# A fused retention and feed-forward kernel: one more token block through a seven-product first matmul, another seven-product scheme for the second, and part of v scaled on GpSimd

## Chip, cores and metric

The kernel runs on one core of one Trainium2 chip. The metric is the device time of one execution in microseconds (us). Before the change it is the median of three runs.

## The reference

A retention layer (8 batches, 8 heads, 576 positions, head dimension 64) and behind it a feed-forward layer with an exact GELU:

```python
scores = scale * np.matmul(q, k.transpose(0, 1, 3, 2))
gamma = 1.0 - 2.0 ** (-5.0 - np.arange(H, dtype=np.float32))
rel = pos[:, None] - pos[None, :]
Dmat = np.where(rel >= 0, gamma[:, None, None] ** rel[None, :, :], 0.0)
attn_out = np.matmul(scores * Dmat[None, :, :, :], v)
x = attn_out.transpose(0, 2, 1, 3).reshape(B * S, H * D)        # 4608 x 512
h = x @ w_in                                                    # w_in 512 x 2048
g = 0.5 * h * (1.0 + erf(h / np.sqrt(2.0)))
out = g @ w_out                                                 # w_out 2048 x 512
```

All arrays come in float32; the kernel works in bfloat16 with float32 sums.

## The kernel before, in words

The 4608 tokens are nine blocks t = 0 to 8 of `TOK` = 512. The retention part is cut into 36 units of 128 tokens, four to a block. A unit goes through these steps: q, k and v are loaded by GpSimd's DMA queue (L318), q and k are transposed (`turn`, L482, on TensorE for the first seven groups, `turn_dma`, L492, by DMAs of SyncE's queue behind that), scores (`sc`, L516 to L535), decay mask on VectorE (`ret`, L554 and L558), the inner product (`o_ps`, L591 and L600), the product with the running state (L653), and the evacuation to `xT` (L672, or L456/L461 for first units). The state `u_ps` (L619) needs v scaled per head (`vh`): `scaled_v` does this on ScalarE for the 15 units listed in `BY_ACT` (eight instructions a unit, L572) and on VectorE for 21 units (one instruction, L575).

**First product** (x by w_in, then GELU). Blocks 0 to 5 use the plain form `mlp1` (L701, tile `hT`): 16 column groups of four matmuls, 64 matmuls of 512 columns a block. From block `FAST` = 6 on, `fast` (L966, tile `f`) does it by a Winograd form: of each pair of column groups four pieces j, of each piece seven products P1 to P7 with four matmuls of 256 columns, so 112 matmuls of 256 columns a block. Its operands are sums of x (`xs`, L939) and of w_in (`wi`, L924 to L926, and L931 in place); its results are joined by VectorE (L981, L985) and passed through GELU on ScalarE (L987, L991). P7 is kept in a float32 tile of its own, `p7`.

**Second product** (g by w_out). Block 0 is plain (`mlp2`, L746, tile `oT`). Blocks 1 to 8 use `part` (L885, tile `m`): seven products M1 to M7 in Strassen's form, each in four steps k of four matmuls of 256 columns. `sum_g` makes three sums of g for each of four pieces j (L782 and L786 with 1024 elements a partition, L784 with 512). `sum_w` makes five sums of w_out (L192 to L195). `after` copies and adds the finished products (L821, L826, L837, L846, L851, L456/L461/L463), and stores the block (`store`, L729).

**Order.** Everything is recorded into the engines' queues by one host loop (`fire` and the `while True` loop behind it). It keeps an estimate of each engine's time in `T`, asks which step is ready, and appends its instructions. So the order of each queue is fixed when the program is built, and on the chip an instruction waits only for its operands and for those ahead of it in its queue. The list `ORDER` gives the order of the loads on GpSimd's queue (`wi1 k1 wi0 io ...`), in which `dq2` to `dq4` (L299) are small GpSimd multiplications that make decay factors; the entries with a plus sign are delays that steer the host loop and issue nothing.

For the last block three products are cut into three pieces (`PIECES`) so that the last stores are small.

Of the kernel before, what the change touches and what calls it, by code (L numbers as in the profile page):

```python
# [9 lines left out]
FP32 = mybir.dt.float32  # L10
BF16 = mybir.dt.bfloat16
# [6 lines left out]
def kernel(  # L18
# [52 lines left out]
    FAST, ALL_FAST = 6, 6  # L71
    N_LD = 5
    N_QKT = 4
# [6 lines left out]
    HOLD = 9  # L80

# [6 lines left out]
    g_pool = ctx.enter_context(tc.tile_pool(name="g", bufs=1))  # L88
# [15 lines left out]
    def on(engine, dur, ready=0.0):  # L104
# [37 lines left out]
    def constants():  # L142
# [7 lines left out]
        far_at = on("dve", 0.55, at)  # L150
        nc.vector.tensor_scalar(ident, val, 0.0, None, op0=ALU.is_equal)
        on("dve", 0.35)
# [6 lines left out]

    N_NEAR, NEAR = 5, (0, 2, 4, 6, 1, 3, 5, 7)  # L160
# [27 lines left out]
    def sum_w(i):  # L188
        w = w_out_sb[i]
        s = w_sum[i] = const.tile([128, 5, 256], BF16, name=f"w_sum{i}")  # L190
        b11, b12, b21, b22 = w[:, 0, 0:256], w[:, 0, 256:512], w[:, 1, 0:256], w[:, 1, 256:512]
# [4 lines left out]
        ws_at[i] = on("dve", 1.05, land_out[i]) + SEM  # L196

# [87 lines left out]
    def load(what, i):  # L285
# [8 lines left out]
        if what == "dq":  # L294
# [6 lines left out]
            dq_at[i] = on("pool", 1.2, dq_at[i - 1])  # L301
# [23 lines left out]
    for x, keys in enumerate(zip(*HW_FIRST)):  # L325
        for n, (what, i) in enumerate(keys):
# [3 lines left out]
    ORDER = ("wi1 k1 wi0 io q1 v0 q2 k2 v1 wi2 v2 k3 wi3 q3 v3 wi4 wi5 wi6 k4 q5 k5 q4 v5 wi7 wo1 wo0 k6 v4 dq2 "  # L330
# [7 lines left out]
             "b21+6.0").split()  # L338

    BY_ACT = {int(x[1:]) for x in ORDER if x[0] == "a"}  # L340
    S_LATE = {int(x[1:].split("+")[0]): float(x.split("+")[1]) for x in ORDER if x[0] == "s"}
    B_LATE = {int(x[1:].split("+")[0]): float(x.split("+")[1]) for x in ORDER if x[0] == "b"}
    DVE_LAG, P_WAIT, HURRY = ({int(x[1:].split("+")[0]): float(x.split("+")[1]) for x in ORDER if x[0] == kind} for kind in "zpu")
    ORDER = [x for x in ORDER if x[0] not in "abszpu"]
# [76 lines left out]
    DRAIN = 0.25  # L421
    SEM = 0.12
# [140 lines left out]
    def scaled_v(i):  # L563
# [5 lines left out]
        by_act = i in BY_ACT  # L569
        if by_act:  # L570
            for h in range(H):
                nc.scalar.activation(vh[:, h, :], loaded[i][1][:, h, :], AF.Copy, scale=dv[:, h, ci:ci + 1])  # L572
            st[i]["V"] = on("act", 2.0, at) + SEM
        else:
            nc.vector.tensor_tensor(vh, loaded[i][1], dv[:, :, ci:ci + 1].to_broadcast([128, H, D]), op=ALU.mult)  # L575
            st[i]["V"] = on("dve", 0.685, at) + SEM
# [109 lines left out]
    def g_of(t, mm):  # L686
        return g_tiles[t, mm // 2][:, mm % 2] if t else g_tiles[t, mm // 2][mm % 2]

    def g_done(t, j):
        if t > 0 and all((t, 4 * j + x, ts) in g_at for x in range(4) for ts in range(4)):  # L690
            at = max(g_at[t, 4 * j + x, ts] for x in range(4) for ts in range(4)) - SEM
            for x in range(3):
                queued.append((at, x, sum_g, (t, j, x)))
# [654 lines left out]
```

## Time and profile before

| | before |
|---|---|
| median of 3 runs | 285.56 us (285.5 to 286.11) |
| span of the profiled execution | 283.7 us |
| median less that span | 1.9 us |
| TensorE matmuls busy | 278.0 us (98%) |
| VectorE busy | 199.7 us (70%) |
| ScalarE busy | 158.8 us (56%) |
| GpSimd busy | 114.0 us (40%) |
| matmuls | 3361 |

The profile gives no other time for the profiled execution than its span, from the first to the last instruction. What lies around it is taken as the 1.9 us between that span and the median. PE is TensorE's matmuls, PEld its weight loads, DVE VectorE, ACT ScalarE, POOL GpSimd, SP SyncE; a q behind the name means the engine's sequencer, which issues DMAs. In rows of the groups, "busy, mean ns of one | idle before" follow the count.

### The profile page before, as it was taken

How to read it: one execution, taken by the hardware profiler on the slowest of the kernel's cores; microseconds unless marked ns; L12 is line 12 of the kernel's file. 1: busy time of each engine (PE TensorE's matmuls, PEld its weight loads, DVE VectorE, ACT ScalarE, POOL GpSimd, SP SyncE). 2: the span in 40 equal slices, each digit the busy share in tenths (PEclk: the TensorE clock that was granted, in tenths of full speed). 3: DMA queues.
4: the chain of work that ended last, by engine and by line, in shares of the span. 5: the costliest groups of instructions: out<-in, count | busy, mean ns of one | idle time of the engine just before them, and what ended most of it. 6: DMA issues, size and time to landing. Idle time of an engine off the chain costs nothing.

```text
span 283.7 us, 8075 instructions
## 1 busy us (share of the span) xinstructions
PE 278.0 (98%) x3361; PEld 207.6 (73%) x3361; DVE 199.7 (70%) x412; ACT 158.8 (56%) x362; POOL 114.0 (40%) x143
## 2 busy tenths in 40 slices
PE   8989999999999999999999999999999999999994
PEld 3577666688874588548855778558888888888894
DVE  5753483979865595898178867889669968966822
ACT  5676724755456635693298874564565374665320
POOL 8979987993364465625468552000000000000000
PEclk9999999999999999999999999999999999999999
DMA  9999999999999999999999999910003000400133
GB/s 150 165 182 173 188 180 163 146 142 147 172 161 195 190 147 128 156 229 149 135 197 203 147 137 150 222 21 2 0 2 128 23 2 0 151 0 2 74 114 111
DMA packets 152804, 35.39 MB, mean 125 GB/s; under 512 B 141120, under 2 KB 148928, under 8 KB 152768
## 3 DMA queue, kind: packets, MB, share of 16 engines
q0 software_dynamic: 116832, 18.10, 95.3%
q1 hardware_dynamic: 34528, 16.26, 32.9%
q10 hardware_dynamic: 1408, 0.52, 0.7%
q8 instruction: 26, 0.43, 0.7%
q14 instruction: 10, 0.08, 0.1%
HBM read 36.70 MB, written 9.44 MB: 163 GB/s over the span
## 4 chain that ended last, share of the span: by engine, by line
PE 92%; POOL 3%; DMA 3%; issue 0%; DVE 0%; POOLq 0%
PE m L885 35%; PE hT L701 29%; PE f L966 13%; PE oT L746 5%; PE o_ps L600 3%; PE sc L535 3%; DMA w_in<-in_moe_w_in_dram 3%; POOL qk L318 2%; PE o_ps L653 1%; PE u_ps L619 1%; PE qk_ps L482 1%; POOL v_ld L318 1%; POOL w_in L291 1%; PE sc L525 0%; PE o_ps L591 0%
## 5 line engine op out<-in xcount | busy, mean ns | idle before, releaser
L701 PE MATMUL hT<-xT,w_in 128*128 128x512 bf16 (+3 forms) x560 | 87.4, 312 | 0.8 <-DMA w_in<-in_moe_w_in_dram 0.8
L710 ACT ACTIVATE g<-hT 128x512 bf16<-128x512 f32 (+2 forms) x106 | 57.7, 556 | 36.9 <-PE hT L701 36.1
L701 PEld LDWEIGHTS <-w_in 128*128 128x128 bf16 x560 | 48.4, 98 | 33.8 <-DMA w_in<-in_moe_w_in_dram 1.0
L885 PEld LDWEIGHTS <-gs 128*128 128x128 bf16 x656 | 62.2, 98 | 7.7
L885 PE MATMUL m<-w_sum,gs 128*128 128x256 bf16 (+1 forms) x400 | 47.7, 268 | 0.0
L318 POOL DMA_DIRECT2D v_ld<-in_v_dram x40 | 34.0, 854 | 19.3 <-DMA qk_ld<-in_k_dram 8.8
L318 POOL DMA_DIRECT2D qk_ld<-in_k_dram x36 | 30.4, 851 | 21.7 <-DMA qk_ld<-in_q_dram 19.1
L558 DVE TENSOR_TENSOR ret<-sc,msk 128x512 bf16<-128x512 f32 x48 | 30.2, 683 | 12.2 <-PE sc L535 12.2
L318 POOL DMA_DIRECT2D qk_ld<-in_q_dram x36 | 30.4, 851 | 16.9 <-DMA qkT<-qk_ld 6.5
L885 PE MATMUL m<-w_out,gs 128*128 128x256 bf16 x256 | 32.5, 273 | 0.0
L885 PE MATMUL m<-w_sum,g 128*128 128x256 bf16 x256 | 30.9, 273 | 0.0
L572 ACT ACTIVATE vh<-v_ld,dv 128x64 bf16<-128x64 bf16 x120 | 30.0, 339 | 0.0
L782 DVE TENSOR_TENSOR gs<-g 128x1024 bf16<-128x1024 bf16 x32 | 21.8, 686 | 9.0 <-ACT g L710 8.2
L885 PEld LDWEIGHTS <-g 128*128 128x128 bf16 x256 | 24.9, 98 | 3.9
L991 ACT ACTIVATE g<-f 128x512 bf16<-128x512 f32 x36 | 20.2, 590 | 8.9 <-PE f L966 7.5
L786 DVE TENSOR_TENSOR gs<-g 128x1024 bf16<-128x1024 bf16 x32 | 21.6, 684 | 0.0
L672 DVE TENSOR_TENSOR xT<-o_ps,dqT 128x512 bf16<-128x512 f32 (+1 forms) x32 | 18.4, 617 | 4.5 <-PE o_ps L653 4.4
L966 PEld LDWEIGHTS <-w_in 128*128 128x128 bf16 x192 | 18.8, 98 | 2.2
L461 ACT CAST u_sb<-u_ps 128x512 bf16<-128x512 f32 x15 | 8.7, 587 | 16.0 <-PE u_ps L619 16.0
L461 ACT COPY o<-m 128x512 f32<-128x512 f32 x14 | 8.2, 587 | 15.7 <-PE m L885 15.7
L987 ACT ACTIVATE g<-p 128x512 bf16<-128x512 f32 x12 | 7.6, 630 | 14.1 <-DVE p L985 14.1
L966 PEld LDWEIGHTS <-wi 128*128 128x128 bf16 x144 | 14.0, 98 | 1.6
(96 smaller groups left out, 337.6 us busy)
## 6 DMA issues: line engine op xcount, KB each, us to landing
out_dram<-o SPq DMA_DIRECT2D x27, 256.0 KB, 6.3
v_ld<-in_v_dram POOLq DMA_DIRECT2D x32, 128.0 KB, 9.1
qk_ld<-in_k_dram POOLq DMA_DIRECT2D x28, 128.0 KB, 10.7
qk_ld<-in_q_dram POOLq DMA_DIRECT2D x28, 128.0 KB, 8.6
w_in<-in_moe_w_in_dram POOLq DMA_DIRECT2D x8, 256.0 KB, 7.3
w_out<-in_moe_w_out_dram POOLq DMA_DIRECT2D x8, 256.0 KB, 8.0
out_dram<-o SPq DMA_DIRECT2D x14, 128.0 KB, 2.1
qk_ld<-in_q_dram POOLq DMA_DIRECT2D x8, 64.0 KB, 11.4
```

The source lines that it names most:

```text
L318: nc.gpsimd.dma_start(dst, src[2 * bp + jj, :, ci * C:ci * C + n, :].rearrange("h s d -> s h d"))
L461: nc.scalar.copy(dst, src)
L558: nc.vector.tensor_tensor(r, t, by, op=ALU.mult)
L572: nc.scalar.activation(vh[:, h, :], loaded[i][1][:, h, :], AF.Copy, scale=dv[:, h, ci:ci + 1])
L672: nc.vector.tensor_tensor(x_of(i)[:, :, n * x:n * x + n], o, dqT[:, :, ci * C:ci * C + n], op=ALU.mult)
L701: nc.tensor.matmul(hT[:, m, :], lhsT=w[:, cc, o:o + 128], rhs=x_tiles[t][:, cc, lo:hi], start=(cc == 0), stop=(cc == N_DM - 1))
L710: nc.scalar.activation(g_of(t, m0 // 2)[:, m0 % 2:m0 % 2 + n, lo:hi], hT, AF.Gelu)
L782: nc.vector.tensor_tensor(s.rearrange("p m a b -> p m (a b)"), g[:, :, 0, :], g[:, :, 1, :], op=ALU.add)
L786: nc.vector.tensor_tensor(s, g[:, :, :, LEFT], g[:, :, :, RIGHT], op=MINUS)
L885: nc.tensor.matmul(m[:, 0 if apart else ts, :], lhsT=a, rhs=w[:, c0:c1], start=p in begins and mm == 0 and ts == 0, stop=mm == N_DF // 2 - ...
L966: nc.tensor.matmul(m[:, y, :], lhsT=a[:, c], rhs=d[:, c], start=p in (P1, P7) and y == 0 and c == 0, stop=c == 1, skip_group_check=True)
L991: nc.scalar.activation(g[:, :, rows, cols], m, AF.Gelu)
```

## The change

1. `FAST` goes from 6 to 5: block 5 also uses the Winograd form of the first product.
2. The second product of blocks 1 to 8 goes over to the same Winograd form: seven products Q1 to Q7, four sums of g (`S1` to `S4`, where S2 is made from S1 and S4 from S2), four sums of each w_out tile in place of five. Q1, Q6, Q5 and Q3 add up in one PSUM bank, one behind the other, with a copy or an addition between them; Q7 and Q4 share a second bank; Q2 adds to a copy of Q1. In the queue they stand as Q1, Q7, Q6, Q4, Q2, Q5, Q3.
3. g lies in three buffers of two pieces each (`N_G`) in place of four buffers of one; P7 is kept in the part of the g tile that is still free, so the tile `p7` goes.
4. Eight units' v are scaled on GpSimd (`BY_POOL`: 32, 31, 3, 14, 7, 24, 15, 19) with one instruction each, five on ScalarE, 23 on VectorE.
5. The host loop's costs know of GpSimd operations that meet VectorE operations with two SBUF inputs (`port`, `pairs_read`), the first transposes wait for the identity (`const_at`), and `ORDER` is another list.
6. For the last block Q1, Q6, Q5 and Q3 are all cut into the three pieces, in place of M1 and M7.

```diff
-    FAST, ALL_FAST = 6, 6
+    FAST, ALL_FAST = 5, 5
+    N_G = 3
+    POOL_V = 1.1
...
-    g_pool = ctx.enter_context(tc.tile_pool(name="g", bufs=1))
+    g_pool = ctx.enter_context(tc.tile_pool(name="g", bufs=N_G))
...
+    def on(engine, dur, ready=0.0, pair=False):
         lap = 0.075 if engine == "dve" and dur > 0.2 else 0.0
-        T[engine] = max(T[engine], ready) + dur - lap
+        start = max(T[engine], ready)
+        if pair:
+            for a, b in port[-2:]:
+                if a < start + dur and start < b:
+                    start = max(start, b - 0.1)
...
     def sum_w(i):
-        s = w_sum[i] = const.tile([128, 5, 256], BF16, name=f"w_sum{i}")
-        nc.vector.tensor_tensor(s[:, 0], b11, b22, op=ALU.add)
-        nc.vector.tensor_tensor(s[:, 1], b12, b22, op=MINUS)
-        nc.vector.tensor_tensor(s[:, 2], b21, b11, op=MINUS)
-        nc.vector.tensor_tensor(s[:, 3:5], w[:, :, 0:256], w[:, :, 256:512], op=ALU.add)
+        s = w_sum[i] = const.tile([128, 4, 256], BF16, name=f"w_sum{i}")
+        nc.vector.tensor_tensor(s[:, 0], w[:, 0, 256:512], w[:, 0, 0:256], op=MINUS)
+        nc.vector.tensor_tensor(s[:, 1], w[:, 1, 256:512], w[:, 0, 256:512], op=MINUS)
+        nc.vector.tensor_tensor(t2, w[:, 1, 256:512], t1, op=MINUS)
+        nc.vector.tensor_tensor(t4, w[:, 1, 0:256], t2, op=MINUS)
...
-    ORDER = ("wi1 k1 wi0 io q1 v0 q2 k2 v1 wi2 v2 k3 wi3 q3 v3 wi4 wi5 wi6 k4 q5 k5 q4 v5 wi7 wo1 wo0 k6 v4 dq2 "
+    ORDER = ("wi1 k1 wi0 io q1 v0 q2 k2 v1 wi2 v2 k3 wi3 q3 v3 wi4 wi5 q4 wi6 dq2 k5 dq3 q5 k4 wi7 v4 wo0 wo1 v5 "
...
+        if i in BY_POOL:
+            nc.gpsimd.tensor_tensor(vh, loaded[i][1], dv[:, :, ci:ci + 1].to_broadcast([128, H, D]), op=ALU.mult)
+            st[i]["V"] = on("pool", POOL_V, at) + SEM
...
-    bank_of = {M3: "X", M4: "Y", M5: "X", M1: "Z", M2: "Y", M6: "V", M7: "Z"}
+    bank_of = {Q1: "X", Q6: "X", Q5: "X", Q3: "X", Q7: "V", Q4: "V", Q2: "Y"}
-    behind = {M5: M3, M1: M4, M2: M4, M6: M1, M7: M1}
+    behind = {Q6: Q1, Q2: Q1, Q4: Q7, Q5: "C21", Q3: "C22"}
...
-    def sum_g(t, j, n):
-            nc.vector.tensor_tensor(s.rearrange("p m a b -> p m (a b)"), g[:, :, 0, :], g[:, :, 1, :], op=ALU.add)
-            nc.vector.tensor_tensor(s[:, :, 0], g[:, :, 0, LEFT], g[:, :, 1, RIGHT], op=ALU.add)
-            nc.vector.tensor_tensor(s, g[:, :, :, LEFT], g[:, :, :, RIGHT], op=MINUS)
+    def sum_g(t, js, n):
+        a11, a12, a21, a22 = g[:, :, 0, LEFT], g[:, :, 1, LEFT], g[:, :, 0, RIGHT], g[:, :, 1, RIGHT]
+        o, a, b, op = {S1: (s1, a21, a22, ALU.add), S2: (s2, s1, a11, MINUS), S3: (s3, a11, a21, MINUS), S4: (s4, a12, s2, MINUS)}[n]
+        nc.vector.tensor_tensor(o, a, b, op=op)
...
+        if p == Q1:
+            return g[:, 0, a], w[:, 0, LEFT]
+        if p == Q2:
+            return g[:, 1, a], w[:, 1, LEFT]
+        if p == Q4:
+            return g[:, 1, b], ws[:, 3]
+        s = gs_tiles[t, mm // 4, sum_of[p]][:, mm % 4, a]
+        return s, w[:, 1, RIGHT] if p == Q3 else ws[:, {Q5: 0, Q7: 1, Q6: 2}[p]]
...
+        if p == Q1:
+            at = either(dur, done, held_bank[t, "Y", 0][1][:, xs, c0:c1], m)
+        elif p == Q7:
+            seen(t, Q7, 0, either(dur, max(done, o_at(t, 1)), hi[:, :, RIGHT], m))
+        elif p == Q2:
+            at = either(dur, max(done, o_at(t, 0)), lo[:, :, LEFT], m)
+        elif p == Q4:
+            at = either(dur, max(done, o_at(t, 1)), hi[:, :, LEFT], m)
+        elif p == Q3:
+            at = either(dur, done, lo[:, xs, 256 + c0:256 + c1], m)
...
+    def add_out(t, n, what, done, ready):
+        d = 256 * (what == "C22")
+        nc.vector.tensor_tensor(hi[:, xs, d + c0:d + c1], m, hi[:, xs, d + c0:d + c1], op=ALU.add)
...
-                p7_tiles.append(ld_pool.tile([128, 2, 2, 256], FP32, tag="qk", bufs=N_LD, name="p7"))
-            f_bank[key, "p7"] = p7_tiles[0][:, j % 2]
+            f_bank[key, "p7"] = g.rearrange("p m a b -> p m (a b)")[:, :, 256:768].bitcast(FP32)
...
+    SEQ = (Q1, Q7, Q6, Q4, Q5, Q3)
+    FILL = ((Q5, (0, 1, 2, 3)),)
...
-            runs.append([("3", t, p, k) for p in range(7) for k in range(4)])
+            order = [(p, k) for p in SEQ for k in range(4) if p != Q2]
+            for at, ks in FILL if t < N_BLK - 1 else ((Q5, range(4)),):
+                n = order.index((at, 0)) if at is not None else len(order)
+                order[n:n] = [(Q2, k) for k in ks]
+            runs.append([("3", t, p, k) for p, k in order])
```

Counted in the built programs (before to after): TensorE matmuls 3361 to 3447; of these `hT` 560 to 520 (of 512 columns 264 to 192, of 384 24 to 16, of 256 136 to 152, of 128 136 to 160), `f` 336 to 448, `m` 880 to 864 of 256 columns and 32 to 64 of 128, `warm` 33 to 31. VectorE: sums of g 96 to 72, joins of `f` 24 to 32, copies and additions of `m` 35 to 28. ScalarE: `vh` 120 to 40 instructions. GpSimd: `vh` 0 to 8 instructions. The bytes of all loads and stores are the same.

More of the change, by code (lines that the diff above doesn't have):

```diff
@@ L857, in after @@
-        if last and p == M5:
-            for x in range(2):
-                store(t, x, lo[:, x, RIGHT], 256, 512)
-        if last and p == M2:
-            for x in range(2):
-                store(t, 2 + x, hi[:, x, LEFT], 0, 256)
-        read_at[t, p] = at + SEM
+        piece = last and p in CHAIN
+        b, m = held_bank[t, bank_of[p], n if piece else 0]
+        xs, c0, c1 = pieces(t)[n] if piece else (slice(0, 2), 0, 256)
+        dur = 0.15 + 0.00104 * (xs.stop - xs.start) * (c1 - c0)
@@ new lines, in add_out @@
+    def add_out(t, n, what, done, ready):
+        hi = o_tiles[t, 1]
+        last = t == N_BLK - 1
+        b, m = held_bank[t, "X", n]
+        xs, c0, c1 = pieces(t)[n]
+        d = 256 * (what == "C22")
+        nc.vector.tensor_tensor(hi[:, xs, d + c0:d + c1], m, hi[:, xs, d + c0:d + c1], op=ALU.add)
+        seen(t, what, n, on("dve", 0.15 + 0.00104 * (xs.stop - xs.start) * (c1 - c0), max(done, ready)))
+        if last and n != 1:
+            x = xs.start
+            store(t, 2 + x, hi[:, x, d:d + 256], d, d + 256, *((nc.scalar, nc.scalar) if n else ()))
+        elif what == "C22" and not last:
+            for x in range(2):
+                store(t, 2 + x, hi[:, x, :])
@@ L968, in fast @@
         done = pe(4 * 0.1092, 4)
-        g = g_tiles[key]
+        g = g_part(t, j)
         if p == P1:
@@ L1072, in lead @@
     def lead():
-        while runs and not (runs[0] and heads(runs[0])):
-            runs.pop(0)
+        n = 0
+        while n < min(3, len(runs)):
+            if runs[n] and heads(runs[n]):
+                n += 1
+            else:
+                runs.pop(n)
         one = heads(runs[0])[0][0] if runs else None
```

272 lines of the change are left out of this document (150 added, 122 removed), and 14 rows, old and new, of the table ORDER.

## The prediction

> **What bounds the kernel now.** I read the page's totals and its slices first, then what the matmul engine waited for, then the chain that ended last in order of time, then the groups by shape and the stretches.
>
> ```profile
> span 283.7 us, 8075 instructions
> PE 278.0 (98%) x3361; PEld 207.6 (73%) x3361; DVE 199.7 (70%) x412; ACT 158.8 (56%) x362; POOL 114.0 (40%) x143
> ...
> PEclk9999999999999999999999999999999999999999
> DMA  9999999999999999999999999910003000400133
> ```
>
> TensorE is busy for 98% at the full clock. The DMA engines are just as full for 26 of 40 slices, so "who bounds" is settled by the waits: matmul engine only, columns are total us, times, longest.
>
> ```profile
> PE warm L1187 <- DVE zeros L118: 1.2, 1, 1.2
> PE hT L701 <- DMA w_in<-in_moe_w_in_dram: 0.8, 1, 0.8
> ```
>
> After the start it waited once, 0.8 us, for a load. The chain (start us, us, what) shows when, and the pace of the stream:
>
> ```profile
> 11.04 7.39 DMA w_in<-in_moe_w_in_dram
> 18.47 1.05 PE hT L701 x8
> 97.95 0.97 PE hT L701 x4
> 113.59 5.18 PE hT L701 x24
> 222.61 0.98 PE m L885 x8
> 229.75 2.62 PE f L966 x24
> 263.37 16.65 PE m L885 x168
> 280.04 0.29 DVE o L846
> ```
>
> The w_in tile `wi3`, issued at 11.04, opens a gate at 18.47; from there to 280.04 the chain is one stream of matmuls, 261.6 us, and the rest is the last addition, stores and the end. So until something breaks the stream, the time changes by what TensorE's work changes, and work taken off VectorE, ScalarE or GpSimd is worth nothing by itself.
>
> **Block 5's first product.** It goes from 64 matmuls of 512 columns (5.18 / 24 = 0.2158 us each, 13.81 us) to 112 of 256 (2.62 / 24 = 0.1092 us, 12.23 us): -1.58 us. All of it lies on the stream.
>
> **Finer cuts.** Two of the half-wide matmuls take 0.2184 us against 0.2158 for one of full width: 0.0026 us for each further matmul. In blocks 0 and 1 the same columns are cut into 24 more (-8 of 512, -8 of 384, +16 of 256, +24 of 128), in the last block `m` into 16 more: +0.10 us. The second product has seven products of 16 matmuls a block before and after, so the new scheme itself removes none.
>
> **Changes of the array's shape.** Four `hT` after retention matmuls take 0.97 us against 4 x 0.2158 = 0.86, eight `m` 0.98 against 0.87: 0.11 us for each change of shape. Between full array, row, column and quarter tiles the queue changes 78 times before and 79 times after: +0.11 us.
>
> **The gate.** GpSimd's queue issues the same loads in the same order up to `wi5`, past `wi3`, so the gate stays. Three more idle matmuls stand ahead of the first transposes, and later ones fall away (two fewer in all). At most three of the start's would be late, 3 x 0.445 us:
>
> ```profile
> 1.20 4.45 PE L1187 MATMUL warm<-zeros 128*128 128x512 bf16 x10 [1.20 <-DVE zeros L118]
> 19.10 0.89 POOL L318 DMA_DIRECT2D qk_ld<-in_k_dram  x1 [1.49 <-DMA w_in<-in_moe_w_in_dram]
> ```
>
> That is 1.3 us, of which the 0.8 us of waiting covers most: 0 to +0.5, and no gain, as the load sets the gate. I take 0: other idle matmuls were removed behind them.
>
> **GpSimd's queue.** `dq2` and `dq3` now stand between `wi6`, `k5` and `q5`, `q4` goes ahead of `wi6`. Rows for this and for the vector work (groups by shape: busy, mean ns | idle before):
>
> ```profile
> L299 POOL TENSOR_TENSOR dqT<-dqT,step 128x512 f32<-128x512 f32 x2 | 2.1, 1058 | 0.0
> L572 ACT ACTIVATE vh<-v_ld,dv 128x64 bf16<-128x64 bf16 x120 | 30.0, 339 | 0.0
> L575 DVE TENSOR_TENSOR vh<-v_ld,dv 128x512 bf16<-128x512 bf16 x21 | 14.3, 700 | 0.0
> L782 DVE TENSOR_TENSOR gs<-g 128x1024 bf16<-128x1024 bf16 x32 | 21.8, 686 | 9.0 <-ACT g L710 8.2 <-PE m L885 0.7
> L784 DVE TENSOR_TENSOR gs<-g 128x512 bf16<-128x512 bf16 x32 | 13.4, 419 | 0.1
> L786 DVE TENSOR_TENSOR gs<-g 128x1024 bf16<-128x1024 bf16 x32 | 21.6, 684 | 0.0
> L851 DVE TENSOR_TENSOR o<-m,o 128x512 f32<-128x512 f32 x7 | 4.8, 684 | 1.0 <-PE m L885 1.0
> L981 DVE TENSOR_TENSOR f<-p,f 128x512 f32<-128x512 f32 x12 | 8.3, 694 | 4.7 <-ACT p L461 3.3 <-ACT g L987 0.7 <-PE f L966 0.5
> L558 DVE TENSOR_TENSOR ret<-sc,msk 128x512 bf16<-128x512 f32 x48 | 30.2, 683 | 12.2 <-PE sc L535 12.2
> L672 DVE TENSOR_TENSOR xT<-o_ps,dqT 128x512 bf16<-128x512 f32 x24 | 15.4, 683 | 1.3 <-PE o_ps L653 1.2
> L939 DVE TENSOR_TENSOR xs<-xT,xs 128x512 bf16<-128x512 bf16 x6 | 2.5, 422 | 0.1
> ```
>
> The two take 2 x 1.06 us, but the queue sat 1.49 us at that place until a transfer was through, since it runs ahead of the transfers. What is left is 0.63 us on the issues behind (`k5`, `q5`, `k4`, `wi7`, the w_out tiles), with transfers still queued ahead of them: 0 to +0.63, taken as 0. The eight `vh` on GpSimd have no row; the nearest is `dqT`'s, as many elements with two inputs: 1.06 us each, 8.5 us within the 26 slices (184 us) of full DMA engines; behind each wait the next loads, with the same cover.
>
> **VectorE and ScalarE** off the path: sums of g fall from 56.8 us (21.8 + 13.4 + 21.6) to 56 x 0.685 + 16 x 0.419 = 45.1; eight joins more of `f`, +5.5; seven operations fewer on `m`, -4.8; four `xs`, +1.7; two `vh`, +1.4: 199.7 becomes some 192 us. ScalarE loses 80 of 120 `vh`, 20 us. Cost on the path 0, hidden by the stream; without that cover, see the first rival. Where GpSimd's and VectorE's work meet:
>
> ```profile
> 50.93 0.65 POOL L299 TENSOR_TENSOR dqT<-dqT,step 128x256 f32<-128x256 f32 x1
> 51.09 1.05 DVE L575 TENSOR_TENSOR vh<-v_ld,dv 128x512 bf16<-128x512 bf16 x1
> ```
>
> The `vh` took 1.05 instead of 0.70 us beside a GpSimd multiplication. Eight of 1.06 us hold VectorE by 0 to 8.5 us in all; even so it ends at 200, where it was.
>
> **New waits in the second product.** Q6 waits for Q1's copy behind all of Q7 (16 x 0.109 = 1.75 us), Q4 for Q7's behind Q6, Q5 for a copy and an addition behind Q2: each such step lasts under 1.75 us by L851's 0.684 and a hand-over. Between Q5 and Q3 no step of the block stands. A group of four takes 0.60 us where its stream takes 0.44, so the result is some 0.16 us late:
>
> ```profile
> 258.41 0.60 PE L966 MATMUL f<-xs,w_in 128*128 128x256 bf16 x4
> ```
>
> The wait is thus 0.16 + 0.684 and two hand-overs of under 0.1, about 1.0 us. In the recorded queue 1.3 us or more of other matmuls lie there in blocks 1 to 6, but eight (0.87 us) in block 7: +0.13 us. In block 8 the three pieces follow each other and cover it. From the last group of `f` on, block 8's sums (16 x 0.419 = 6.7 us at most) run beside Q3 of block 7, Q1 and Q7 (5.3 us) and Q6 needs the fourteenth: 0 to +0.6, taken as 0, as successive sums overlap.
>
> **The end.** The last piece is again 128 columns wide, one VectorE operation (0.29 us, now a copy) and one store: 0, within 0.3 either way.
>
> **Sum:** -1.58 + 0.10 + 0.11 + 0.13 = -1.24 us on a span of 283.7, so 282.5. The median stands 1.9 us above the span; 285.56 - 1.24 = **284.3 us**.
>
> **A rule against the step.** Of half-wide matmuls the Trainium skill, "TensorE: Matmul & The Clock Gate", section "Back-to-back issue gap", says that in a sustained stream of weight loads and matmuls one takes about 81 ns at 128 columns and 131 ns at 512, so half the width is far from half the time. Estimated from that page (98 ns at 256, on a straight line), block 5 would go from 8.4 to 11.0 us, 2.6 us longer, and the sum would be 288.5. The rows above (0.2158 and 0.1092) disagree with it.
>
> **Rivals.** *VectorE becomes the bound where block 5's new form meets the retention units (slower).* Stretches of the profile (us, busy of PE, PEld, DVE, ACT, POOL, then clock, DMA share, GB/s):
>
> ```profile
> 160.00:180.00 20.00, 20.00 (x264) 14.87 (x261) 14.68 (x30) 12.99 (x40) 6.40 (x9) 1.00 1.99 148
> 180.00:200.00 20.00, 20.00 (x275) 14.00 (x275) 18.12 (x36) 10.10 (x18) 0.00 (x0) 1.00 0.31 65
> 200.00:220.00 20.00, 20.00 (x222) 17.73 (x220) 14.69 (x27) 11.97 (x22) 0.00 (x0) 1.00 0.13 49
> ```
>
> and one pair of units on the chain:
>
> ```profile
> 80.36 0.57 PE o_ps L600 x16
> 80.92 0.25 PE u_ps L619 x16
> 81.18 0.35 PE o_ps L653 x16
> 81.52 0.45 PE sc L535 x32
> ```
>
> A block with both forms and four units costs VectorE 8 joins (5.5), 8 sums (5.5), 4 `xs` (1.7), 8 masks (5.5), 4 `xT` (2.7), some 2.6 `vh` (1.8) and 5 copies and additions at 0.69 (3.5): 26.2 us. TensorE needs 224 x 0.109 = 24.4 and, for two pairs of units at 1.62 with a change of shape or two, about 3.5. So 26.2 against 27.9; two meetings with GpSimd at 1.06 us make 28.3. For it: 18.12 of 20 at 180 to 200. Against it: that stretch cost TensorE nothing, and operations in a row overlap. It decides from about 19 of 20 us in a stretch. Late masks then hold the inner products; two to three such blocks at about 1 us: 284.3 + 2.5 = 286.8 us, chance 0.17. By the Trainium skill, "SBUF — State Buffer", section "Practical consequences", the later of a GpSimd operation that reads SBUF and a VectorE one with two inputs there is blocked fully; the trace's 0.35 us is of that kind.
>
> *Hand-overs eat it (no change).* If all eight blocks and the three other handed-on products lose like block 7, 8 x 0.13 = 1.0 us goes: 285.3 us. Or the full DMA engines rather than TensorE set the stage of block 5, so that the 1.58 us don't arrive and the change does not do what it says: 285.9. Against both: the single wait of 0.8 us. Together 0.16.
>
> *Short groups pay their ends (slower).* If each group of four cost its 0.60 us in full, block 5 would take 28 x 0.60 = 16.8 us, 3.0 more than before: 288.9 us. Against it: the six such groups at 229.75 ran at 0.109. Chance 0.01. The rule of the Trainium skill above is of this kind.
>
> **How the numbers follow.** A measurement of this kernel tells some 0.2% (0.57 us) from no change. The forecast, with late loads (+0.63) and late sums still in it, ends between 283.6 (no lost hand-over, the end 0.3 us shorter) and 284.9; chance 0.66. Range 283.6 to 286.3: it takes in the second rival and the shallow part of the first, and leaves out its deeper part, 0.13, and a few hundredths at either end. Faster 0.66, same 0.16, slower 0.18.
>
> **What would show it.** Right: `f` x448 at 0.109 us, TensorE's waits still near 1 us behind the gate, the gate at 18.5, VectorE near 192 us, eight `vh` on POOL near 1.06 us. Wrong: TensorE waiting for VectorE at `o_ps`, `f` or `m` for over 1 us in all, a stretch with VectorE above 19 of 20, a gate past 19, or waits for w_in or w_out behind it.

## The result, and the profile after

The changed kernel takes **288.73 us** (median of six runs, 287.67 to 290.44) against 285.67 us (285.50 to 286.35) for the kernel before on the same chip: ratio 1.0114, 95% interval 1.0086 to 1.0141. It is 3.1 us slower, outside the range of 283.6 to 286.3; 284.3 was forecast. Medians here and below are of all runs; ratios and intervals leave out runs more than 1.5% above the fastest of the same kernel. The profile is of the fastest of the six, so it shows 2.2 of the 3.1 us. Its totals and two of its slice rows:

```profile
span 285.9 us, 8160 instructions
PE 277.2 (97%) x3447; PEld 212.9 (74%) x3447; DVE 200.8 (70%) x400; ACT 146.9 (51%) x294; POOL 122.4 (43%) x151
...
PE   8989999999999999999999899999998999999995
...
DMA  9999999999999999999999999991021000400215
```

TensorE's row now has 8s in the middle; before it was solid. DMA is full one slice longer. What TensorE waited for (total us, times, longest):

```profile
PE m L943 <- ACT g L1050: 1.3, 1, 1.3
PE warm L1267 <- DVE zeros L134: 1.2, 1, 1.2
PE o_ps L672 <- issue: 1.2, 1, 1.2
PE qk_ps L499 <- DMA qk<-in_q_dram: 0.7, 1, 0.7
PE f L1027 <- DVE f L1040: 0.3, 1, 0.3
PE o_ps L610 <- DVE vh L594: 0.3, 1, 0.3
PE qk_ps L499 <- ACT g L741: 0.2, 1, 0.2
```

Before, the 0.8 us at the gate was the only entry after the start. From the matmul records I count a *hole* wherever two matmuls start over 25 ns further apart than is usual for their shape, from 18 us on: 4.5 us in all here, none before. The last matmul starts at 282.33 us against 279.79. Without its holes it would start at 277.8, 2.0 us earlier than before. Not all of that is removed work. The matmuls up to the first transposes behind the gate are the same in both kernels, but for two idle ones, and these transposes start 0.7 us earlier in this profile, because another load opened them (before's rows, then the changed kernel's):

```profile
18.47 1.05 PE L701 MATMUL hT<-xT,w_in 128*128 128x256 bf16 x8 [0.78 <-DMA w_in<-in_moe_w_in_dram]
19.36 0.61 PE L482 MATMUL qk_ps<-ident,qk 128*128 128x128 bf16 x8
```

```profile
16.85 1.05 PE L737 MATMUL hT<-xT,w_in 128*128 128x256 bf16 x8
18.63 0.62 PE L499 MATMUL qk_ps<-ident,qk 128*128 128x128 bf16 x8 [0.74 <-DMA qk<-in_q_dram]
```

From there to the last matmul before took 260.4 us, and the changed kernel 259.2 without its holes: 1.2 us of work are gone, and the holes cost more than three times that. The longest, on ScalarE, VectorE and TensorE in order of time (start us, us, ..., [idle before <-releaser]):

```profile
212.77 0.58 ACT L478 COPY f<-f 128x512 f32<-128x512 f32 x1
215.96 0.60 ACT L1050 ACTIVATE g<-f 128x512 bf16<-128x512 f32 x1 [2.60 <-DVE f L1040]
```

```profile
213.85 0.68 DVE L820 TENSOR_TENSOR gs<-g 128x1024 bf16<-128x1024 bf16 x1
214.56 0.69 DVE L820 TENSOR_TENSOR gs<-gs,g 128x1024 bf16<-128x1024 bf16 x1
215.18 0.69 DVE L1040 TENSOR_TENSOR f<-g,f 128x512 f32<-128x512 f32 x1
```

```profile
214.70 0.60 PE L1027 MATMUL f<-xs,wi 128*128 128x256 bf16 x4
216.60 0.60 PE L943 MATMUL m<-w_out,g 128*128 128x256 bf16 x4 [1.30 <-ACT g L1050]
```

ScalarE stands idle for 2.6 us ahead of P2's GELU until VectorE's addition for **P6** (L1040) is through, though P2's GELU reads only its own bank. VectorE is busy with sums of g. Then the GELU runs, and only then TensorE's `m`. The group of these GELUs, before's first, shows that this isn't one accident: `x` count | busy, mean ns | idle before:

```profile
L991 ACT ACTIVATE g<-f 128x512 bf16<-128x512 f32 x36 | 20.2, 590 | 8.9 <-PE f L966 7.5 <-DVE f L981 1.4
```

```profile
L1050 ACT ACTIVATE g<-f 128x512 bf16<-128x512 f32 x48 | 27.2, 595 | 19.4 <-DVE f L1040 16.0 <-PE f L1027 2.6
L820 DVE TENSOR_TENSOR gs<-g,gs 128x1024 bf16<-128x1024 bf16 x14 | 10.8, 775 | 0.5
L996 DVE TENSOR_TENSOR w_in<-w_in 128x256 bf16<-128x256 bf16 x8 | 3.8, 488 | 1.0 <-PE hT L737 0.9
```

Before, the same group idled 1.4 us behind that addition (two GELUs), now 16.0 (12 of the 16 P2 GELUs). The program says why: P7 now lies in columns 256 to 767 of each row of the g piece, P2's GELU writes columns 0 to 255 of the same rows. The two don't overlap, but their rows interleave, and the GELU is made to wait for the P6 addition that reads P7.

The theories: **A**, this wait through the shared tile; **B**, TensorE's instructions arrive late (the 1.2 us at `o_ps` whose releaser is only "issue", in the middle of 16 matmuls that depend on nothing new); **C**, VectorE's load; **D**, GpSimd's scaling of v, by meeting VectorE's sums or by coming late.

### The profile page after: what moved, and what is told of

Its sections match the earlier page's. It is cut to its first block, busy times and chain, and to the rows that moved or that the text cites. A ratio compares the mean times of both kernels' runs of the same rounds, so it can differ in the third digit from the quotient of the medians.

```text
span 285.9 us, 8160 instructions
## 1 busy us (share of the span) xinstructions
PE 277.2 (97%) x3447; PEld 212.9 (74%) x3447; DVE 200.8 (70%) x400; ACT 146.9 (51%) x294; POOL 122.4 (43%) x151
## 3 DMA queue, kind: packets, MB, share of 16 engines
HBM read 36.70 MB, written 9.44 MB: 161 GB/s over the span
## 4 chain that ended last, share of the span: by engine, by line
PE 85%; DVE 6%; POOL 4%; DMA 2%; issue 1%; ACT 1%; POOLq 0%; DVEq 0%; ACTq 0%
PE m L943 33%; PE hT L737 22%; PE f L1027 16%; PE oT L777 5%; PE sc L552 3%; PE o_ps L619 3%; DMA qk<-in_q_dram 2%; DVE gs L820 2%; POOL qk L336 2%; PE qk_ps L499 1%; PE o_ps L672 1%; PE u_ps L638 1%; DVE xT L691 1%; POOL w_in L309 1%; DVE ret L571 1%
## 5 line engine op out<-in xcount | busy, mean ns | idle before, releaser
L737 PE MATMUL hT<-xT,w_in 128*128 128x512 bf16 (+3 forms) x520 | 73.9, 297 | 0.0
L943 PEld LDWEIGHTS <-gs 128*128 128x128 bf16 x536 | 49.8, 98 | 7.0
L943 PEld LDWEIGHTS <-g 128*128 128x128 bf16 x392 | 37.4, 98 | 6.6 <-issue 1.5
L943 PE MATMUL m<-w_out,g 128*128 128x256 bf16 (+1 forms) x264 | 33.1, 269 | 1.3 <-ACT g L1050 1.3
L820 DVE TENSOR_TENSOR gs<-g 128x1024 bf16<-128x1024 bf16 (+1 forms) x36 | 20.9, 624 | 3.7 <-ACT g L741 3.7
L912 DVE TENSOR_TENSOR o<-m,o 128x512 f32<-128x512 f32 (+2 forms) x20 | 11.5, 582 | 16.2 <-ACT o L478 9.9
L1027 PE MATMUL f<-xs,wi 128*128 128x256 bf16 x128 | 19.2, 272 | 0.3 <-DVE f L1040 0.3
L1027 PE MATMUL f<-xs,w_in 128*128 128x256 bf16 x128 | 19.1, 273 | 0.0
L1027 PE MATMUL f<-xT,w_in 128*128 128x256 bf16 x128 | 18.9, 273 | 0.0
L1046 ACT ACTIVATE g<-g 128x512 bf16<-128x512 f32 x16 | 10.1, 630 | 13.8 <-DVE g L1044 13.8
```

What stands on the lines that cost most here:

```text
L737: nc.tensor.matmul(hT[:, m, :], lhsT=w[:, cc, o:o + 128], rhs=x_tiles[t][:, cc, lo:hi], start=(cc == 0), stop=(cc == N_DM - 1))
L820: nc.vector.tensor_tensor(o, a, b, op=op)
L912: nc.vector.tensor_tensor(hi[:, xs, d + c0:d + c1], m, hi[:, xs, d + c0:d + c1], op=ALU.add)
L943: nc.tensor.matmul(m[:, 0 if apart else ts, :], lhsT=a, rhs=w[:, c0:c1], start=p in begins and mm == 0 and (ts == 0 or apart), stop=mm == ...
L1027: nc.tensor.matmul(m[:, y, :], lhsT=a[:, c], rhs=d[:, c], start=p in (P1, P7) and y == 0 and c == 0, stop=c == 1, skip_group_check=True)
```

## The experiments

Each is timed beside the kernel before on its chip. Unless said otherwise TensorE's order is that of the changed kernel.

**1. p7 out of P2's way (A).** The g tile is stored quadrant by quadrant:

```diff
-g_pool.tile([128, 4, 2, TOK], ...)              # mm, row, columns
+g_pool.tile([128, 2, 2, 2, 2, 256], ...)        # piece, row, half, mm, columns
-f_bank[key, "p7"] = g.rearrange("p m a b -> p m (a b)")[:, :, 256:768].bitcast(FP32)
+f_bank[key, "p7"] = g.rearrange("p r h m c -> p (r h m c)")[:, 512:1536].bitcast(FP32)...
```

> The changed kernel with one thing moved: a block's g tile is stored quadrant by quadrant, so that the seventh product's sum (p7), which lies in g, and the quadrant that P2's GELU writes no longer interleave in memory. Every engine's order is that of the changed kernel; only ScalarE's wait for VectorE's P6 addition ahead of each P2 GELU is gone. Theory A (ScalarE held by VectorE through the shared tile: in the changed kernel the group g<-f of L1050 was idle 16.0 us for f of L1040, 12 times): the 1.47 us hole in TensorE at 215.0 and the 0.48 us at 225.0 go, median 286.5 to 287.3 us against 288.7. Theory B (TensorE's instruction packets come late behind the loads: the 1.32 us hole at 158.6 with no releaser but issue): the median stays at 288.2 to 288.7, and the spread of nearly 3 us over the runs stays. Theory C (VectorE itself is the bound at 180 to 216): the wait comes back behind another VectorE sum, 288 or more.

Measured 287.44 us (ratio 1.0045, 1.0025 to 1.0065; the changed kernel's interval begins at 1.0086), just above the 286.5 to 287.3 that A gave. The GELU group and the waits:

```profile
L1059 ACT ACTIVATE g<-f 128x512 bf16<-128x512 f32 x48 | 27.2, 596 | 11.0 <-PE f L1036 9.0 <-DVE f L1049 1.4
```

```profile
PE m L952 <- DVE gs L830: 0.6, 1, 0.6
...
PE f L1036 <- DVE f L1049: 0.3, 1, 0.3
PE o_ps L610 <- DVE vh L594: 0.3, 1, 0.3
PE o_ps L672 <- issue: 0.2, 1, 0.2
```

The 16.0 us are back to 1.4 and the hole at 215 is gone. A is shown, worth 0.7% by the ratios (1.3 us by the medians). The hole at 224, which I had put to A too, stays at 0.48 us.

**2. Longer rows in the loads (B).**

```diff
-nc.gpsimd.dma_start(dst, src[2 * bp + jj, :, ci * C:ci * C + n, :].rearrange("h s d -> s h d"))
+nc.gpsimd.dma_start(to, rows)      # units 4 on: 128 rows of 2 KB, one behind the other
```

> The changed kernel, with the q, k and v loads of units 4 on (the short ones of single rows apart) reading 2 KB rows that lie one behind the other, instead of 256-byte rows: as many bytes, an eighth of the packets, and other elements of q, k and v, so the values are not the reference's. Orders on every engine are unchanged. Theory B (late instruction packets behind full DMA engines): the hole at 158.6 goes, instruction packets land within 5 us of the matmul that I take to ask for them (8.0 and 8.4 us at the worst in the changed kernel), median 286.3 to 287.5 us, spread under 1 us. Theory A (the wait through the g tile) or C (VectorE the bound): 288.2 to 288.7, and the hole at 215 stays at 1 to 1.5 us.

Measured 289.37 us (1.0114, 1.0087 to 1.0142): no gain, and B's median and spread (1.6 us) missed. The hole at 158.6 did go, as B says: its instruction packet landed at 154.8 in this profile, 4.1 us before it was needed. But the loads came earlier and GpSimd's `vh` with them: two of them (1.07 us at 164.15, 1.11 at 166.30) fell beside a `gs` sum (1.62 us in place of 0.69) and `w_in` (1.14 in place of 0.28). P5's addition came 1.3 us later, and TensorE waited:

```profile
PE f L1033 <- DVE g L1050: 1.9, 1, 1.9
PE m L949 <- ACT g L1056: 1.3, 1, 1.3
```

The profiled run, the longest of the five (290.18 us), also lost some 1.7 us behind that wait to a lower clock (an estimate: 4 us at 0.57, last section). The edit moved more than it tested: D's mechanism showed itself, B stayed open.

**3. Both.** 

> Both edits of this call in one kernel: p7 clear of P2's quadrant, and long rows in the loads (other elements of q, k and v). If A and B are both true and add up, 284.0 to 285.5 us: the matmul stream is 2.3 us shorter than before's and little is left to wait for. If one of them is true, as its own kernel. If VectorE bounds the stage (C), 287 or more.

288.45 us (1.0079, 1.0049 to 1.0110): the 1.3 us of A are gone, the 1.9 us behind P5's addition are still there. The two don't add to what I expected.

**4. First product from block 6 again** (`FAST, ALL_FAST = 6, 6`). 

> The changed kernel with the first product by seven products from block 6, as before, and not from block 5: the second product's four sums, GpSimd's share of v and the recorded order stay, and the order from block 5 on is planned anew. By the prediction's steps block 5's seven products are worth 1.58 us, so without any new wait this is 286.0 us. If block 5's first product brings the waits (12 VectorE instructions of 0.4 to 0.7 us in the stretch 180:200, which stood at 19.45 of 20 us; theory C), it is faster than the changed kernel: 286.0 to 287.0. If the second product's scheme and GpSimd's part bring them, it is as slow or slower: 288.7 to 290.3.

290.56 us (1.0167, 1.0136 to 1.0198). It is above all that was expected, and tells little: the order from block 5 on is planned anew and has waits of its own (0.9 us of `sc` for a GELU, 0.7 us of `hT` for `ret`).

**5. v on VectorE (D, C).**

```diff
-nc.gpsimd.tensor_tensor(vh, loaded[i][1], ...)
+nc.vector.tensor_tensor(vh, loaded[i][1], ...)
```

> The changed kernel with the eight parts of v that GpSimd scales scaled by VectorE instead, at the same places of the recorded order: VectorE gets 8 x 0.68 = 5.4 us more, GpSimd loses 8 x 1.07 us. Theory D (GpSimd's scaling of v meets VectorE's sums of two SBUF inputs, both take longer, and where the meeting falls depends on when a load lands, so some runs wait more): the spread over the runs of nearly 3 us shrinks to about 1 us and the median falls to 287.0 to 288.0 us; the 1.3 to 1.5 us wait of m of L943 for a GELU stays. Theory C (VectorE's load itself is the bound): 289.5 or more, because 5.4 us come on top, two of the eight in the stretch that stood at 19.45 of 20 us. Theory B (late instruction packets): unchanged, 288.2 to 289.2, with the spread.

> p7 clear of P2's quadrant (as in the run at 287.44 us) and the eight parts of v scaled by VectorE. If A and D hold and add: 285.5 to 286.3 us with a spread under 1 us. If C holds, VectorE's 5.4 us more shows as waits of TensorE for VectorE at 180 to 216, 288 or more. If only A holds: 287.2 to 287.8.

Alone 290.37 us (1.0116, 1.0076 to 1.0157), with p7 apart 287.88 us (1.0046, 1.0021 to 1.0071). Alone it is 1.6 us slower than the changed kernel by the medians, but by the ratios no difference shows, either way. The traces show an exchange. With p7 apart and GpSimd's v, VectorE's rows have a meeting at 102.8, beside a `vh` of 1.46 us on GpSimd, and TensorE a hole of 0.72 us behind it:

```profile
102.78 1.42 DVE L830 TENSOR_TENSOR gs<-gs,g 128x1024 bf16<-128x1024 bf16 x1
104.23 0.69 DVE L830 TENSOR_TENSOR gs<-g,gs 128x1024 bf16<-128x1024 bf16 x1
```

```profile
102.19 1.46 POOL L587 TENSOR_TENSOR vh<-v_ld,dv 128x512 bf16<-128x512 bf16 x1
```

With v on VectorE that hole is 0.15 us, but units 31 and 32 stand ahead of a sum that TensorE needs at 191, a hole of 0.90 us:

```profile
190.21 1.28 DVE L588 TENSOR_TENSOR vh<-v_ld,dv 128x512 bf16<-128x512 bf16 x2
191.41 1.89 DVE L834 TENSOR_TENSOR gs<-g 128x1024 bf16<-128x1024 bf16 x3
```

**6. The late four on ScalarE.** 

> As the one before, but the four parts of v of units 19, 24, 31 and 32 go to ScalarE (eight activations each, as others of the kernel), since VectorE is fullest from 140 us on; the four early ones go to VectorE. D without C: as the one before, within 0.4 us. C: faster than it by 1 us or more. ScalarE stood at 51% busy; if its 2.7 us a unit hold up evictions there, 0.5 to 1 us slower than the one before.

289.07 us (1.0104, 1.0066 to 1.0142), 1.2 us slower than all on VectorE. ScalarE's order suffered: the sum at 193.60 waited 2.48 us for a GELU, and TensorE's hole there grew to 1.99 us.

**7. The other way round: the kernel before with those eight v on GpSimd.** 

> The kernel before with the v of the same eight units (3, 7, 14, 15, 19, 24, 31, 32) scaled by GpSimd, and nothing else: five of them were VectorE's and three ScalarE's; TensorE's order is before's. Theory D: GpSimd's instructions meet VectorE's sums there too, 285.8 to 287.5 us with a wider spread than 285.4 to 286.1. The other theories: 285.4 to 285.8, as before, since before's TensorE hardly waits and VectorE is relieved of 3.4 us.

285.97 us (0.9989, 0.9965 to 1.0013). No difference: D is not a cost of GpSimd's v as such. In this profile one of the eight met a VectorE instruction with two inputs (a `w_sum` of 0.28 us took 1.14), none a sum of g, and TensorE waited for none of them.

**8. Lighter sums (C).**

```diff
-nc.vector.tensor_tensor(o, a, b, op=op)
+nc.vector.tensor_copy(o, a12 if n == S4 else a11)      # for S2 and S4
```

> p7 clear of P2's quadrant, and in place of the second product's S2 and S4 a copy of g's quadrant by VectorE: as many instructions on the same tiles in the same order, but with one input and without the chain S1, S2, S4, so VectorE has less to do (S2 and S4 took 0.69 us each from start to start) and the output is not the reference's. Theory C (VectorE is the bound at 180 to 216 once the shared tile is out of the way; there a wait of 0.9 us of m for gs at 191 stood in the runs with p7 apart): that wait goes, 286.0 to 286.9 us against 287.4. Theory B (instruction packets late) or D (meetings): 287.2 to 287.8, with holes at TensorE's chunk ends (matmuls 2007 and 2390) or at a meeting.

> The changed kernel (p7 in the shared tile, GpSimd's v, the loads as they are) with S2 and S4 as copies alone. Theory A says that TensorE waits for ScalarE, which waits for VectorE's addition; a lighter VectorE makes that addition earlier, so the hole of 1.47 us at 215 shrinks to under 0.7: 287.3 to 288.0 us. If VectorE's load is no part of it (A by place alone): 288.3 to 288.9.

With p7 apart 285.55 us (0.9979, 0.9957 to 1.0002), in the changed kernel as it is 287.18 us (1.0051, 1.0028 to 1.0074). Both gain some 0.65%, and between the two A is again worth 0.7%, as between the two runs of experiment 5; between experiments 2 and 3 it is 0.35%. The copies take 0.46 us in the mean, and read one tile where the sums read two. With p7 apart the holes at 69, 103 and 224 go from 0.36, 0.72 and 0.48 us to 0.12, 0 and 0.10; without it the 1.47 us at 215 is still 1.07, as A says. The hole at 191 that I named did not exist here: it belongs to v on VectorE.

**9. No meeting, emptier queues, and all at once.** 

> p7 clear of P2's quadrant, the eight parts of v on VectorE, and 2 KB rows in the loads (other elements of q, k and v, so not the reference's values). GpSimd no longer meets VectorE's sums, and the DMA engines are emptier when TensorE's instructions are fetched. What is left is VectorE's load (C): a wait for gs near 191 of about 1 us, 285.8 to 286.8 us. If B and D were nothing: as with p7 apart alone, 287.2 to 287.9.

> All at once: p7 apart, v on VectorE, 2 KB rows, S2 and S4 as copies (not the reference's values). If the four causes account for the whole loss, TensorE's matmuls run as densely as in the kernel before and the prediction's sum comes out: 284.0 to 284.9 us. If it stays at 286 or more, something else costs: the work on TensorE itself or a load.

287.54 us (1.0070, 1.0042 to 1.0099) and 285.58 us (0.9999, 0.9973 to 1.0025); both missed what was expected (284.0 to 284.9 of the second), and the first stands where it should if B and D were nothing. The second's profile still has the 0.90 us at 191 (v on VectorE) and a hole of 1.26 us at 68.6, behind an instruction packet that took from 62.9 to 67.9 us. Long rows did not make all packets prompt.

**10. VectorE relieved of P5's and P6's additions, in block 5 and in block 8 (C, and the first rival's place).**

```diff
-nc.vector.tensor_tensor(to[1], f_bank[key, "p7"], m, op=ALU.add)
+nc.scalar.copy(to[1], m)                                 # P6, in one block
-nc.vector.tensor_tensor(v, v, m, op=ALU.add)
+v = m                                                    # P5, in the same block
```

> p7 clear of P2's quadrant, and in block 5 alone VectorE's two additions of p7 left out: ScalarE copies P6's bank instead of VectorE adding to it, and P5's GELU reads its bank straight (so block 5's values are not the reference's). VectorE loses 8 x 0.68 = 5.4 us in the stage where it stood at 19 of 20 us. If VectorE's load in block 5's stage is what is left of the loss (C in block 5): 285.5 to 286.5 us against 287.4. If it decides elsewhere: 287.0 to 287.8.

> The same leaving out, in block 8 in place of block 5 (block 8's values are not the reference's). VectorE has room there (11.5 to 16 us of 20 after 200 us), so by C in block 5 this gives nothing: 287.1 to 287.8 us. If what costs is the waiting on VectorE's additions as such, wherever they are, it gains as much as block 5's.

286.99 us (1.0041, 1.0014 to 1.0068) and 286.55 us (1.0034, 1.0009 to 1.0059): neither differs from p7 apart alone (1.0045), nor from the other, within some 0.3%. So VectorE's total load in block 5's stage is not what is left, as far as this can tell; in each the four P6 additions came back as copies on ScalarE. The profile of block 8's is of a run of 288.77 us, 2.2 over its median, and shows what such a run has:

```profile
159.28 0.28 PE L672 MATMUL o_ps<-qkT,u_sb 64*64 64x128 bf16 x3
161.37 0.36 PE L672 MATMUL o_ps<-qkT,u_sb 64*64 64x128 bf16 x11 [1.81 <-issue]
```

**11. A quarter of the load packets left out (B).** (A fifth of the bytes read: 29.36 MB in place of 36.70.)

```diff
-nc.gpsimd.dma_start(dst, ...)
+if what != "v" or i < 8: nc.gpsimd.dma_start(dst, ...)   # later v: a part of w_out
```

> p7 apart, S2 and S4 as copies, and no v loads from unit 8 on (v is taken from a part of w_out that is in the chip, so not the reference's values): 28 of the 36 loads of v are gone, about a quarter of the load traffic, and 28 issues of 0.86 us on GpSimd. Theory B (TensorE's instruction packets wait behind the loads): no hole without a releaser at a chunk end, and the runs lie within 0.8 us of each other at 283.7 to 284.6 us. If B is nothing, the spread stays as with p7 apart and copies (284.2 to 287.3) around 285.5.

287.19 us (1.0035, 1.0017 to 1.0053), 285.92 to 287.73. No hole without a releaser, and none of 12 runs far out; but the median is 1.6 us above that of the same kernel with its loads. New waits stand in it (1.20 us at 49.5 for `ret`, 0.78 at 165.8 for `f`); I read them as work that moved up when it no longer waited for loads, which is not shown. Whether fewer loads cure B can't be separated from that.

**12. Versions that compute the whole.**

```diff
+if i in (33, 34): nc.gpsimd.tensor_tensor(vh, ...)       # e9, beside the eight
-S2: (s2, s1, a11, MINUS)
+S2: (s2, a22, s3, MINUS)                                 # all three
+(nc.gpsimd if i > 30 else nc.vector).tensor_tensor(vh, ...)   # e10, e11
```

> A version that computes the whole: p7 clear of P2's quadrant; the v of units 33 and 34, which VectorE scaled at 201 us in its fullest stretch, on GpSimd, which has nothing to do from 181 us on (2 x 0.64 us off VectorE); and S2 as a22 - S3, which is the same sum without reading the sum just made (0.09 us each). If VectorE's load from 189 to 205 us is what is left (C in block 5): 286.0 to 287.0 us; to beat the kernel before it would have to be under 285.4. If GpSimd's two instructions meet VectorE's sums: 287.4 or more.

> Computes the whole. p7 clear of P2's quadrant; S2 as a22 - S3; of the eight parts of v that the changed kernel gives to GpSimd, units 31 and 32 stay there and the six earlier ones go to VectorE. Theory D (meetings and lateness on GpSimd cost where sums are near, VectorE's load where it is full): no hole at 103 over 0.2 us, none at 158 for GpSimd, none at 191, and the median at 285.6 to 286.6 us. If the place of v does not matter: 287.2 to 287.8, as with p7 apart alone. To beat the kernel before it has to come under 285.4.

> As the one before, with the sum S2 of block 6's second half and P6's addition exchanged on VectorE, so that the addition for which TensorE waits at 224 is 0.6 us earlier. That hole of 0.48 us (0.36 with S2 as a22 - S3) goes: 0.3 to 0.4 us faster than the one before, 285.2 to 286.2 us. If the sum that is now later is waited for instead, no difference.

The first: 287.34 us (1.0035, 1.0007 to 1.0064). Its profile, of a run of 290.4 us, 3.0 over its median, shows D's other face. GpSimd works in order; one unit's `vh` stood behind loads that waited for buffers, and TensorE waited 3.1 us at 158:

```profile
PE o_ps L623 <- POOL vh L591: 3.6, 2, 3.1
```

The second: 286.15 us (1.0021, 0.9998 to 1.0043). The third: **285.55 us** (0.9996, 0.9981 to 1.0011), against 285.56 for the kernel before: it wins back the 3.1 us and does not beat the kernel before. Its waits:

```profile
PE qk_ps L499 <- DMA qk<-in_q_dram: 0.7, 1, 0.7
PE oT L785 <- issue: 0.3, 2, 0.2
PE hT L737 <- DMA w_in<-in_moe_w_in_dram: 0.2, 1, 0.2
PE o_ps L610 <- DVE vh L594: 0.2, 1, 0.2
```

No `m` and no `f` is left in them. (The two `oT` entries are each as long as one matmul, whose record the trace lacks.) The larger holes behind 60 us over the kernels, in us (up to three more of 0.13 to 0.18 us ahead of `f`, at 220, 242 and 251 in the changed kernel, are left out):

```
hole at, waited for             changed   1: p7   8: p7 and   5: v on   e10    e11
                                kernel    apart   copies      VectorE
 69  o_ps for vh (VectorE)       0.36      0.36     0.12       0.36    0.24   0.24
103  m for gs (VectorE)           -        0.72      -         0.15    0.15   0.15
158  o_ps, no releaser           1.32       -        -         1.20    0.89    -
186  o_ps, no releaser            -        0.40     0.40       1.08    0.27    -
192  m for gs                     -         -        -         0.90     -      -
215  m for P2's GELU             1.47       -        -         1.47     -      -
224  f for P6's addition         0.48      0.48     0.10       0.49    0.36    -
```

(Column 5 is v on VectorE with the shared tile.) The exchange of two VectorE instructions in e11 took the hole at 224 away, as expected.

## Why the prediction was wrong

**Block 5's first product, the finer cuts, the changes of shape: right together.** -1.37 us was the sum. From the transposes behind the gate to the last matmul, without the holes, it is -1.2 us in the changed kernel and with p7 apart alike (260.4 us before, 259.2 in both). The groups of four `f` still start 0.44 us apart (214.26, 214.70), so neither *A rule against the step* (288.5) nor *Short groups* (288.9) is borne out: that both come near the measured 288.7 is luck.

**The gate: right in its time, not in what opens it.** In the changed kernel's profile `wi3` held nothing up, and TensorE waited 0.7 us for a load of q, to 18.63. With p7 apart `wi3` opens it at 18.54, as forecast. "No gain" was thus 0.7 us off in the first profile, by when a load landed.

**GpSimd's queue and the `vh`: the durations right, the place wrong.** 1.06 us a piece was forecast and 1.06 to 1.15 measured. "The same cover" was wrong: a `vh` is not only ahead of loads, it is also wanted by TensorE, in order (experiment 12: 3.1 us in one run).

**The step that failed: "VectorE and ScalarE off the path ... cost on the path 0, hidden by the stream".** Two things were wrong in it.

First, it priced VectorE by its total and gave the total as free. The total itself was 200.8 us, not 192: four meetings added 4.7 us (the longest a `w_in` of 1.92 us in place of 0.28), and successive instructions overlapped by 19.9 us in all in place of 23.8. But what a stream needs is each result in time. Only a few VectorE instructions are on time's edge: at 224 one that TensorE wants stands behind sums of g that it does not want yet, at 69 one at the end of 6 us of VectorE work without a gap, which begins with sums; at 103, with p7 apart, it is a sum, lengthened by a meeting. Lightening the sums was worth some 1.9 us (experiment 8); taking 5.4 us off VectorE elsewhere, nothing that shows (experiment 10). That the sums cost by lateness and not by load is shown for the hole at 224 (experiment 12's exchange), and argued for the others.

Second, no step priced the edit that moved `p7` into the g tile. It removes no instruction and its only effect on the program is a wait, P2's GELU behind P6's addition. What is queued behind an added wait pays for it; here this is ScalarE's queue, with the banks that it frees for TensorE: 0.7% (experiment 1).

**New waits in the second product: right.** The one hand-over that was charged, Q3 behind Q5's addition in block 7 (+0.13 us), shows 0.07 us at 268.7; the others, and the late sums of block 8 taken as 0, show none.

**The end: right in the changed kernel, too narrow in e11.** From last matmul to end it was 3.93 us before, 3.56 in the changed kernel, 4.63 in e11. The last store is issued 0.58 us behind the last matmul before and in the changed kernel alike; the 0.37 us between them lie in the program's closing steps, whose last two stand 1.00 us apart before and 0.55 in the changed kernel's profile, and 0.55 too in that of experiment 7, which is the kernel before but for v. In e11 the last store is issued 1.28 us behind. There an earlier store's issue on ScalarE took 1.33 us in place of 0.60 in the changed kernel, and the copy and the stores behind it came later:

```profile
275.84 1.33 ACTq L768 DMA_DIRECT2D out_dram<-o  x1
277.26 0.59 ACT L478 COPY o<-m 128x512 f32<-128x512 f32 x1 [2.95 <-DMA out_dram<-o]
```

So in e11 the last matmul starts 1.04 us earlier than before and the span ends 0.3 us earlier. Why the issue is long in some runs is open.

**The rivals.** *VectorE becomes the bound in block 5's stage* had the sign and part of the size. Its sign for itself held too: 180 to 200 stood at 19.45 of 20 us.

```profile
140.00:160.00 20.00, 18.83 (x295) 11.44 (x297) 17.69 (x32) 10.11 (x17) 12.52 (x14) 1.00 2.02 135
180.00:200.00 20.00, 20.00 (x336) 16.92 (x334) 19.45 (x35) 8.97 (x16) 2.80 (x4) 1.00 1.42 117
200.00:220.00 20.00, 18.70 (x223) 16.46 (x221) 14.74 (x24) 12.15 (x22) 0.00 (x0) 1.00 0.15 54
```

But there TensorE was busy for 20.00 us. It lost time where VectorE stood at 17.69 and 14.74. The decisive point "from about 19 of 20 us" was no such point, and experiment 10 speaks against the place. By the page "SBUF — State Buffer" of the Trainium skill, section "Practical consequences", a VectorE instruction with two SBUF inputs contends with a GpSimd one that reads SBUF; the trace agrees (0.69 becomes 1.42 us at 102.78). A meeting alone decides little: in the changed kernel a sum met at 102.19 took 1.91 us, and TensorE did not wait. *Hand-overs* are ruled out by the table of holes.

**What I had no rival for: TensorE's own instructions.** The holes without a releaser all end 1.2 to 2.1 us after an instruction packet (queue 8) has landed, in the DMA records: changed kernel, TensorE at the spot at 158.56, packet landed 158.73, on again at 159.94; block 8 relieved 159.34, 159.83, 161.37; v on VectorE 158.85, 158.64, 160.11; e10 158.59, 158.19, 159.54. Queue 8 brings one packet for some 128 matmuls (27 for 3447), and the spots lie whole multiples of about 127 matmuls apart. At the spots where any profile has such a hole, looked up in all that have this order of TensorE's: with the packet landed under 1.2 us ahead there is always one, of 0.4 us or more; from 1.2 to 1.4 us sometimes; from 1.4 us on none (e11: 157.0, needed at 158.45; p7 apart: 157.0, needed at 159.7). Late packets and holes thus go together in place and time in ten profiles, of which four are given. What makes a packet late is not shown, since experiments 2, 9 and 11 changed other things too. The 2.8 us between the changed kernel's runs fits holes of this kind and of D's, but only profiled runs show theirs; one of the two longest (290.42 us) also has a mean granted clock of 0.992, the others 0.997 to 1.000.

By size: A some 0.7% and the sums of g some 0.65% are 3.9 us. To be accounted for are 4.3 us, the loss of 3.1 and the 1.2 us of removed work that did not show. The 0.4 us that are left are less than the intervals can tell; packets and GpSimd have holes enough for them, and I have not taken these away one by one. In the profiled run itself 4.5 us of holes, less 1.2 us of work, 0.7 at the gate and 0.4 in the closing steps, make the 2.2 us by which its span is longer.

## What to carry to other kernels

A busy share says which engine can't be sped past, not which result is late: before calling an engine's work hidden, list the instructions whose results the bounding engine takes next, and what stands ahead of each in its queue. When a buffer is folded into another tile, look up in the compiled program what the neighbours now wait for; interleaved rows can tie two regions that never overlap, and keeping them apart in memory untied them here at no cost. Where a kernel's runs spread by more than its changes are worth, account for the holes of each profile one by one rather than for its totals.

## What the runs showed of the hardware

- TensorE stopped in the middle of independent matmuls where its next instruction packet had landed less than 1.2 us, in some cases less than 1.4 us, before it was needed: holes of 0.3 to 2.0 us, at the same matmul in different kernels.
- One GpSimd multiplication of 1.07 us lengthened a VectorE instruction with two SBUF inputs beside it by 0.4 to 1.6 us (0.69 to 1.42 us at 102.78, 0.28 to 1.92 for a `w_in` in the changed kernel).
- In experiment 2, after a wait of 1.9 us, the granted clock was 0.57 for 4 us; after 3.1 us in experiment 12 it was 0.58, but after waits of 1.8 us in experiments 6 and 10 it stayed at 1.00. Experiment 2:

```profile
166.00:168.50 2.50, 0.61 (x35) 0.57 (x32) 2.50 (x5) 0.31 (x1) 1.11 (x1) 1.00 1.67 146
168.50:172.50 4.00, 4.00 (x50) 2.83 (x49) 2.21 (x4) 3.29 (x11) 0.00 (x0) 0.57 1.64 152
```

- Removing a quarter of the load packets made the kernel slower (285.55 to 287.19 us, ratios 0.9979 and 1.0035): in an order recorded for certain landing times, data that come early can cost.
